# Normalised activations turned by DMA instead of TensorE, chunk bounds in two PSUM banks, and a planner that keeps TensorE in one array shape

## The chip, the cores and the metric

The kernel runs on one core of a Trainium2 chip. The metric is device time in microseconds, median of three runs: 303.88 us before (303.85 to 304.03). One further execution was profiled; it took 304.15 us, of which the trace covers a span of 302.4 us.

## What is computed

Attention with chunk selection, then a gated feed-forward layer (FFN). For q, k, v of shape 4 x 8 x 768 x 64 (batch, heads, tokens, head width), keys are cut into 24 chunks of 32. An upper bound of each query's score with each chunk is made from the chunk's smallest and largest keys:

```
ub = sum_d max(q * k_min, q * k_max)          # per query and chunk
top = the 6 chunks of largest ub, among those not after the query's own
scores = where(chunk in top and key <= query, q k^T / 8, -1e9)
attn = softmax(scores); x = attn v            # heads side by side: 3072 tokens x 512
xn = x / rms(x) * g
out = (silu(xn Wg) * (xn Wv)) Wo              # Wg, Wv: 512 x 1536, Wo: 1536 x 512
```

## The kernel before, in words

Work is cut into 12 blocks: a batch b and a third m of its 768 tokens, so 256 tokens with all 8 heads. `ORDER` lists them (m = 0 of all batches first, m = 2 last); "block 3" is the entry with index 3. Each block goes through:

- loads of k, q, v by DMA on SyncE's queue (SP, `load_qk`, `load_v`; the first block also on ScalarE's);
- `job`, once for each group of four heads: VectorE (DVE) turns k and q in 32x32 pieces, casts go to ScalarE (ACT) or GpSimd (POOL), DVE reduces k to chunk minima and maxima, which are placed in a block-diagonal matrix BD;
- `pick`: TensorE (PE) multiplies BD with q (`upper`, L562, 64x64 array tiles), DVE turns the bounds back (L583), finds the sixth largest and makes a mask; the mask enters the scores as a further matmul (L731);
- scores (L720, four 32-row tiles of the array), exponentials on ACT (L770), causal triangles on POOL (L740), values (L796, whole array), normalisation by the softmax sum on DVE (L815) into `xnat`, 128 tokens x 512;
- `norm`: squares and their sum on ACT (L832), the inverse root on POOL (L838, L840), a scaling by it on DVE or ACT (L848, L850), then the turn so that the 512 features lie on partitions: PE transposes into PSUM (L860, eight 128x128 blocks for 256 tokens), and a copy to `xsT` that multiplies by g, one value per partition (DVE L873 or ACT L869);
- `ffn`: gate and value matmuls (L904, 96 of 256 columns per block), tanh and products on ACT, DVE and POOL, the projection (L941, 24 of 512 columns), the output copy and its store on SP (L963).

PSUM holds two "S" tiles of two banks each, for scores (both are taken by one score operation) and bounds (one), and four "F" banks for everything else. Weights are loaded on POOL's queue in thirds. `HELD` makes the loads of blocks 2 and 3 wait for given thirds of the weights, so that these are not slowed.

The order of all this is not written out. Every operation is recorded with an engine, an assumed duration, what it reads, writes and takes from a pool of buffers, and a due time (`pri`, from `due_attn` and `due_ffn`: block number times `PACE`, attention `LEAD` ahead). `Plan.run` then walks through assumed time; on each engine it takes the operation that can start first, by due time among equals, and emits it. So each engine's instruction order is fixed when the program is built; on the chip each engine runs its list in order and waits where a semaphore is not there yet. Where the planner expects TensorE to wait before 60 us of its time, it puts in matmuls that do nothing but keep it busy (`fill`, L1008), called fillers below. `flex` operations may go to one of two engines, as the planner finds better.

Of the kernel before, what the change touches and what calls it, by code (L numbers as in the profile page):

```python
# [114 lines left out]
class Plan:  # L115
# [3 lines left out]
    SHARES = ("scale", "relu", "bd0", "bd1", "dk", "mk")  # L119
    PATIENT = {}  # L120
    RESERVED = ("hh",)
# [38 lines left out]
    def run(self, in_order=(), fill=None):  # L160
# [62 lines left out]
        while todo:  # L223
            best = None
            for e, c in cand.items():
                if not c:
                    continue
                rows = [(est(o, e), o) for o in c]
                rows = [(t, o) for t, o in rows if t is not None]
                if not rows:  # L230
                    continue
                t0 = max(at[e], min(t for t, o in rows))
                now = sorted(((t, o) for t, o in rows if t <= t0 + 1e-9),
                             key=lambda r: (r[1].pri, r[1].seq))
                t, o = now[0]
                if e in self.PATIENT:
                    soon = [r for r in rows if r[0] <= t0 + self.PATIENT[e]]
                    for t, o in now + sorted(soon, key=lambda r: (r[1].pri, r[1].seq)):
                        end = t + o.alts[e][0] - 0.1
                        if not any(t < r[0] < end and r[1].pri < o.pri - 10 for r in soon):  # L240
                            break
                    t0 = max(t0, t)
                if best is None or (t0, o.pri) < (best[0], best[1].pri):
                    best = (t0, o, e)
# [63 lines left out]
def kernel(  # L308
# [48 lines left out]
    buffers("qT", 3, [P, 2, BLK], FP32)  # L357
    buffers("kb", 20, [P, 2, BLK], BF16)
    buffers("VX", 20, [P, 2, 4, D + 1], BF16)
    buffers("qb", 5, [P, 2, BLK], BF16)  # L360
# [5 lines left out]
    buffers("mto", 3, [P, NG, 4, CH], BF16)  # L366
    buffers("pt", 6, [P, 4, 512], BF16)
    buffers("rden", 3, [P, 4], FP32)
# [14 lines left out]
    chunkrow = sb.tile([P, S], BF16, name="chunkrow")  # L383
    rmsg = sb.tile([P, NP], FP32, name="rmsg")
    eps6 = sb.tile([P, 1], FP32, name="eps6")
    mhalf = sb.tile([P, 1], FP32, name="mhalf")
# [13 lines left out]
    assert sorted(ORDER) == [(b, m) for b in range(B) for m in range(NBLK)]  # L400
    PACE, LEAD = 22.5, 70
    MARGIN = 2.0
    FIRST = 8
    SPLIT = {0, 1}
    APART = {0, 1}
    PACKED = {0, 1, 2}
# [67 lines left out]

    HELD = {2: (("wg", 1), ("wg", 1)), 3: (("wo", 0), ("wo", 1))}

# [25 lines left out]
    def loads_due(i, n):  # L502
        return -500 + 10 * i + n if i < 2 else due_attn(i) - 30 + n

    def load_v(i):
        b, m = ORDER[i]
        key = ("vraw", b, m)
        for e in range(2):
            t0 = BLK * m + P * e
            dma(f"load v{b}{m}{e}", "SP", v[b, :, t0:t0 + P, :].rearrange("a p d -> p a d"),  # L510
                lambda e=e: at(key)[:, e].rearrange("p g a d -> p (g a) d"),
                64, 0.023 if i < 2 else 0.019, loads_due(i, 2), writes=[key],
                takes=[(key, "vraw")] if e == 0 else (),
                behind=[HELD[i][1]] if i in HELD and e == 0 else ())

# [15 lines left out]
    def pick(i, gs):  # L531
# [8 lines left out]
        ub, ubn, m8, mk, mtd, mto = (  # L540
            ("ub", b, m, g0), ("ubn", b, m), ("m8", b, m), ("mk", b, m), ("mtd", b, m), ("mto", b, m))
        new = g0 == 0
# [7 lines left out]
        def bank():  # L550
            return at(ub)[:, :, 0:n * 32 * nj].rearrange("p h (g n) -> p g h n", g=n)

        def upper():
            for k_, g in enumerate(gs):
# [71 lines left out]
    def job(i, g):  # L626
# [117 lines left out]
        for kg in [m] + list(range(m)):  # L744
# [40 lines left out]
        for s in range(2):  # L785
# [36 lines left out]
    def norm(i, toks, base):  # L822
# [14 lines left out]
        def rms():  # L837
# [43 lines left out]
    def ffn(i):  # L881
# [6 lines left out]
        for toks, h0 in pieces:  # L888
# [22 lines left out]
            plan.op(f"tanh{U}.{hp}", "ACT", 0.48, 0.6, lambda th=th, gp=gp: SE.activation(  # L911
                out=at(th), in_=at(gp), func=ACT.Tanh, scale=0.5), pri - 20, reads=[gp], writes=[th],
                takes=[(th, "th")])
            plan.op(f"tg{U}.{hp}", "DVE", 0.6, 0.69, lambda th=th, gp=gp, tg=tg:
                    VE.scalar_tensor_tensor(  # L915
                        out=at(tg), in0=at(th), scalar=1.0, in1=at(gp), op0=ALU.add,
                        op1=ALU.mult), pri - 40, reads=[th, gp], writes=[tg], takes=[(tg, "tg")])
            if (i, h0 // 2) in DIRECT:
                plan.op(f"hh{U}.{hp}", "DVE", 0.6, 0.69, lambda tg=tg, vp=vp, hh=hh: VE.tensor_tensor(
                    out=at(hh), in0=at(tg), in1=at(vp), op=ALU.mult), pri - 30, reads=[tg, vp],  # L920
                    writes=[hh], takes=[(hh, "hh")])
# [7 lines left out]
        for s in whole:  # L929
# [8 lines left out]
            def project(h0, h1, s=s, op=op, part=part):  # L938
                for ht in range(h0, h1):
# [12 lines left out]
            o = plan.op(f"project{i}.{s}+", "PE", 0.216 * 2, 0.216 * 2 + 0.17,  # L952
                        lambda project=project: project(last, NHT), pri - 20,
                        reads=[part(NHT - 1)[0], op], writes=[op])
# [5 lines left out]
                    out=at(ob), in0=at(op), scalar1=0.5, scalar2=None, op0=ALU.mult))},  # L960
                pri - 20, reads=[op], writes=[ob], takes=[(ob, "osb")])
            r0 = b * S + BLK * m + P * s
# [79 lines left out]
```

## Time and profile before

| what | value |
|---|---|
| median of three runs | 303.88 us |
| profiled execution | 304.15 us, span 302.4 us |
| TensorE (PE) | 290.9 us busy, 4703 matmuls |
| VectorE (DVE) | 206.7 us busy, 540 instructions |
| ScalarE (ACT) | 219.8 us busy, 396 instructions |
| GpSimd (POOL) | 165.9 us busy, 293 instructions |
| turns on PE (L860) | 96 matmuls |
| feed-forward matmuls (L904) | 1216, of 256 or 128 columns |
| projection matmuls (L941) | 288 (264 in the trace) |
| bytes moved by DMA | 30.62 MB |

Busy time is the union of an engine's instructions. Matmuls overlap in the array: one row may show 0.27 us while the next starts 0.11 us later, so what a group of matmuls takes is read from start to start. A line of groups reads: source line, engine, operation, output tile <- inputs, shapes, count | busy us, mean ns of one | idle time of the engine just before them and who ended it. A line of waits reads: engine, tile, line <- who ended the wait: total us, times, longest.

### The profile page before, as it was taken

Reading aid. Unit: us, or ns where it says so; the run is one execution under the profiler, and the core shown is the slowest. Engines: PE = TensorE matmul, PEld = TensorE weight load, DVE = VectorE, ACT = ScalarE, POOL = GpSimd, SP = SyncE. Lnnn points to the kernel's source line nnn. Section 1 sums busy time; section 2 is a strip of 40 time slices with the busy share of each in tenths; the row PEclk is TensorE's granted clock in tenths of the full one; section 3 lists DMA queues with packets and bytes.
Section 4 is the critical chain, followed back from the end, with each engine's and each line's share of the span. In section 5 each row is a group of like instructions: output and inputs, shape, how many; then the busy total and the mean of one; then the engine's idle time right before and its main releaser. Section 6 shows DMA issues by size and latency. Waiting matters only on the chain.

```text
span 302.4 us, 11439 instructions
## 1 busy us (share of the span) xinstructions
PE 290.9 (96%) x4703; PEld 222.5 (74%) x4732; DVE 206.7 (68%) x540; ACT 219.8 (73%) x396; POOL 165.9 (55%) x293
## 2 busy tenths in 40 slices
PE   8989899998999999999999999999999999999994
PEld 8656696757958867885886787788588688598671
DVE  7994896888999999899889343384456335256250
ACT  3587886778976899898795896798667498476240
POOL 4797586856684888678779365246414043123130
PEclk9999999999999999999999999999999999999998
DMA  8999994775765657586540100100010110110101
GB/s 190 236 208 229 237 204 113 155 203 124 190 158 145 146 113 183 124 167 165 138 99 4 72 2 2 70 4 3 2 72 2 37 38 2 37 37 0 69 2 69
DMA packets 74835, 30.62 MB, mean 101 GB/s; under 512 B 65568, under 2 KB 70176, under 8 KB 74784
## 3 DMA queue, kind: packets, MB, share of 16 engines
q1 hardware_dynamic: 69184, 24.66, 33.6%
q0 software_dynamic: 4752, 4.72, 9.3%
q8 instruction: 37, 0.61, 0.8%
q10 hardware_dynamic: 848, 0.53, 0.6%
q14 instruction: 14, 0.11, 0.1%
HBM read 28.31 MB, written 6.29 MB: 114 GB/s over the span
## 4 chain that ended last, share of the span: by engine, by line
PE 77%; DMA 9%; DVE 3%; POOL 3%; ACT 2%; issue 2%; SPq 2%; ACTq 0%; DVEq 0%; POOLq 0%
PE F L904 37%; PE F L941 17%; PE F L796 7%; PE S L720 7%; PE S L562 5%; DMA wg<-in_moe_w_gate_dram 4%; DMA kraw<-in_k_dram 3%; PE S L731 3%; DMA qraw<-in_q_dram 2%; SPq L422 2%; PE F L860 1%; POOL hh L926 1%; DVE qT L642 1%; POOL pt L740 1%; DVE kT L642 1%
## 5 line engine op out<-in xcount | busy, mean ns | idle before, releaser
L926 POOL TENSOR_TENSOR hh<-tg,vs 128x512 bf16<-128x512 bf16 x60 | 69.6, 1163 | 69.0 <-ACT vs L923 47.3
L770 ACT ACTIVATE pt<-S 128x1024 bf16<-128x1024 f32 (+3 forms) x104 | 87.2, 861 | 19.7 <-PE S L731 19.3
L915 DVE SCALAR_TENSOR_TENSOR tg<-th,F 128x512 bf16<-128x512 bf16 x72 | 48.8, 681 | 41.1 <-ACT th L911 40.5
L904 PE MATMUL F<-xsT,wv 128*128 128x256 bf16 (+1 forms) x608 | 74.8, 267 | 1.4 <-DMA wv<-in_moe_w_val_dram 0.6
L904 PE MATMUL F<-xsT,wg 128*128 128x256 bf16 (+1 forms) x608 | 74.5, 267 | 0.5 <-DVE xsT L873 0.5
L941 PE MATMUL F<-wo,hh 128*128 128x512 bf16 x264 | 65.2, 379 | 1.6 <-issue 0.3
L904 PEld LDWEIGHTS <-wv 128*128 128x128 bf16 x608 | 55.5, 98 | 9.7 <-issue 1.5
L904 PEld LDWEIGHTS <-wg 128*128 128x128 bf16 x608 | 55.5, 98 | 8.6 <-issue 0.6
L911 ACT ACTIVATE th<-F 128x512 bf16<-128x512 f32 x72 | 43.3, 603 | 12.6 <-PE F L904 12.2
L941 PEld LDWEIGHTS <-hh 128*128 128x128 bf16 x288 | 26.5, 98 | 27.6
L923 ACT ACTIVATE vs<-F 128x512 bf16<-128x512 f32 x60 | 35.9, 612 | 9.4 <-PE F L904 8.2
L740 POOL TENSOR_SCALAR_AFFINE_SELECT pt<-pt 128x512 bf16<-128x512 bf16 x48 | 30.9, 649 | 12.1 <-ACT pt L770 11.5
L720 PE MATMUL S<-qb,kb 32*128 32x256 bf16 (+1 forms) x800 | 32.8, 253 | 0.0
L657 DVE TENSOR_REDUCE kx<-kT 128x16 f32<-128x512 f32 x48 | 30.4, 666 | 0.0
L796 PE MATMUL F<-VX,pt 128*128 128x65 bf16 x672 | 26.3, 194 | 0.6 <-POOL pt L740 0.3
L796 PEld LDWEIGHTS <-pt 128*128 128x128 bf16 x672 | 24.1, 98 | 3.3 <-issue 1.3
L720 PEld LDWEIGHTS <-kb 32*128 32x128 bf16 x800 | 13.6, 92 | 14.2 <-issue 13.5
L959 DVE TENSOR_SCALAR osb<-F 128x512 f32<-128x512 f32 x12 | 8.2, 688 | 23.1 <-PE F L941 23.1
L832 ACT ACTIVATE junk<-xnat 128x512 bf16<-128x512 bf16 x24 | 15.1, 627 | 10.1 <-DVE xnat L815 8.8
L731 PE MATMUL S<-mtd,chunkrow 32*128 32x128 bf16 (+2 forms) x384 | 20.3, 203 | 0.0
L815 DVE TENSOR_TENSOR xnat<-F,rden 128x256 bf16<-128x256 f32 x48 | 19.6, 415 | 0.9
L731 PE MATMUL S<-mto,chunkrow 32*128 32x128 bf16 (+2 forms) x384 | 20.0, 203 | 0.1
(61 smaller groups left out, 359.1 us busy)
## 6 DMA issues: line engine op xcount, KB each, us to landing
vraw<-in_v_dram SPq DMA_DIRECT2D x24, 256.0 KB, 4.0
out_dram<-osb SPq DMA_DIRECT2D x24, 256.0 KB, 2.2
kraw<-in_k_dram SPq DMA_DIRECT2D x72, 64.0 KB, 2.9
qraw<-in_q_dram SPq DMA_DIRECT2D x72, 64.0 KB, 2.4
wg<-in_moe_w_gate_dram POOLq DMA_DIRECT2D x3, 512.0 KB, 10.8
wv<-in_moe_w_val_dram POOLq DMA_DIRECT2D x3, 512.0 KB, 12.6
wo<-in_moe_w_out_dram POOLq DMA_DIRECT2D x3, 512.0 KB, 17.0
kraw<-in_k_dram SPq DMA_DIRECT2D x10, 128.0 KB, 4.7
```

Source lines behind the costliest of these rows:

```text
L657: plan.op(f"ext{n}{J}", "DVE", 0.585, 0.67, lambda n=n, op=op: VE.tensor_reduce(out=at(kx)[:, n], in_=at(kT).rearrange("p h (c t) -> p h c ...
L720: TE.matmul(s[a // 2][:, a % 2, c0:c0 + q1 - q0], kbt[r, t, ks], qbt[r, t, q0:q1], start=(t == 0), stop=(t == 1 and not mask), skip_group_ ...
L731: TE.matmul(o, chunkrow[r, BLK * kg + P * e:BLK * kg + P * (e + 1)], mv, start=False, stop=(d == 1), skip_group_check=True)
L740: GE.affine_select(out=d, in_=d, compare_op=ALU.is_ge, fill=0.0, base=0, pattern=[[0, 4], [1, P]], channel_multiplier=-1)
L770: lambda pt=pt, hs=hs, c0=c0, c1=c1, x=sc[hp]: SE.activation(out=at(pt)[:, hs, c0:c1], in_=at(x)[:, :, c0:c1], func=ACT.Exp, scale=SCALE), ...
L796: TE.matmul(o[:, a, :], p_[:, a, off:off + P], vt[:, e, a, :], start=(kb_ == 0 and a == 0), stop=(kb_ == nkb - 1 and a == 3), skip_group_c ...
L904: TE.matmul(at(p_)[:, n * W:(n + 1) * W], w[:, g, ht * P:(ht + 1) * P], at(xT)[:, g, x0:x0 + W], start=(g == 0), stop=(g == NP - 1), skip_ ...
L911: plan.op(f"tanh{U}.{hp}", "ACT", 0.48, 0.6, lambda th=th, gp=gp: SE.activation(out=at(th), in_=at(gp), func=ACT.Tanh, scale=0.5), pri - 2 ...
L915: VE.scalar_tensor_tensor(out=at(tg), in0=at(th), scalar=1.0, in1=at(gp), op0=ALU.add, op1=ALU.mult), pri - 40, reads=[th, gp], writes=[tg ...
L923: plan.op(f"vcopy{U}.{hp}", "ACT", 0.48, 0.6, lambda vs=vs, vp=vp: SE.activation(out=at(vs), in_=at(vp), func=ACT.Copy), pri + 0.1, reads= ...
L926: plan.op(f"hh{U}.{hp}", "POOL", 1.11, 1.16, lambda tg=tg, vs=vs, hh=hh: GE.tensor_tensor(out=at(hh), in0=at(tg), in1=at(vs), op=ALU.mult) ...
L941: TE.matmul(at(op)[:], at(key)[:, o:o + P], wo[:, ht, :], start=(ht == 0), stop=(ht == NHT - 1))
```

## The change

- From block 3 on (`BYDMA`), `norm` no longer turns on PE. DVE multiplies `xnat` by the inverse root and by g in one instruction; for that g is broadcast over all partitions into a new tile `gB` by a DMA. Then, for each 128 tokens, SP issues a DMA that transposes `xs` into `xsT`. The PSUM tile of the turn and the copy out of it are gone for these blocks.
- The bounds go to two F banks, one for each half of the heads, instead of one S tile; DVE turns them back in two instructions.
- Planner: after a bounds or score operation (`mode` other than "full"), operations of such a mode are preferred by 60 us of due time over those that use the whole array (`STICK`); `PATIENT` lets DVE wait up to 0.6 us for something more urgent; `PACE`, `LEAD` and several due times are different.
- Block 1's two head groups are picked together (`APART`). Block 3's k and q loads wait for the second instead of the first third of Wo. The weights' issues follow a planned operation of block 0 and stay in their order.
- Fewer buffers of kb, VX and pt.

In the instruction lists of the two programs: PE's turn matmuls go from 96 to 24, fillers of 512 columns from 38 to 46, and TensorE changes between array shapes 121 instead of 130 times, 7 of them directly between scores and bounds. DVE gets 18 of the new scalings, loses 6 of the old and 3 copies to `xsT`; ACT loses 12 scalings and 24 copies. SP issues 18 transposes and one load more.

```diff
     SHARES = ("scale", "relu", "bd0", "bd1", "dk", "mk")
-    PATIENT = {}
+    PATIENT = {"DVE": 0.6}
+    STICK = 60
...
                 now = sorted(((t, o) for t, o in rows if t <= t0 + 1e-9),
                              key=lambda r: (r[1].pri, r[1].seq))
+                if e == "PE" and mode not in (None, "full") and self.STICK:
+                    now.sort(key=lambda r: (r[1].pri - (0 if r[1].mode == "full" else self.STICK), r[1].seq))
...
-    buffers("kb", 20, [P, 2, BLK], BF16)
-    buffers("VX", 20, [P, 2, 4, D + 1], BF16)
+    buffers("kb", 18, [P, 2, BLK], BF16)
+    buffers("VX", 19, [P, 2, 4, D + 1], BF16)
...
-    buffers("pt", 6, [P, 4, 512], BF16)
+    buffers("pt", 5, [P, 4, 512], BF16)
...
+    gB = sb.tile([P, DM], FP32, name="gB")
...
-    PACE, LEAD = 22.5, 70
+    PACE, LEAD = 23.0, 60
     MARGIN = 2.0
     FIRST = 8
+    FROM = 3
+    GATES = {"0": "dk(0, 0, 0)", "1": "dk(0, 0, 0)", "2": "dk(0, 0, 0)", "o": "dk(0, 0, 0)"}
     SPLIT = {0, 1}
-    APART = {0, 1}
+    APART = {0}
+    BYDMA = set(range(FROM, len(ORDER)))
...
-    HELD = {2: (("wg", 1), ("wg", 1)), 3: (("wo", 0), ("wo", 1))}
+    HELD = {2: (("wg", 1), ("wg", 1)), 3: (("wo", 1), ("wo", 1))}
...
-        return -500 + 10 * i + n if i < 2 else due_attn(i) - 30 + n
+        return -500 + 10 * i + n if i < 2 else due_attn(i) - 20 + n
...
-            ("ub", b, m, g0), ("ubn", b, m), ("m8", b, m), ("mk", b, m), ("mtd", b, m), ("mto", b, m))
+            [("ub", b, m, g0, h) for h in range(2)], ("ubn", b, m), ("m8", b, m), ("mk", b, m), ("mtd", b, m), ("mto", b, m))
...
-                            TE.matmul(bank()[64 * c:64 * (c + 1), k_, hp],
+                            TE.matmul(bank()[hp][64 * c:64 * (c + 1), k_],
...
-                    upper, base + 3, reads=reads, writes=[ub], takes=[(ub, "S")])
+                    upper, base + 3, reads=reads, writes=ub, takes=[(x, "F") for x in ub])
...
-        plan.op(f"ubn{tag}", "DVE", turned, turned + 0.08, lambda: VE.transpose(out=flat(ubn), in_=bank()),
-                base + 3, reads=[ub], writes=own_(ubn), takes=takes(ubn, "ubn"))
+        def back():
+            for h in range(2):
+                VE.transpose(out=flat(ubn)[:, :, h], in_=bank()[h])
...
-                pri = base + (5 if masked else -4)
+                pri = base + (2 if masked else -4)
...
-            pri = base + (-4 if i in SPLIT and not s else 9)
+            pri = base + (-4 if i in SPLIT and not s else 6)
...
+        if i in BYDMA:
+            for s in toks:
+                xn, xs, tt = ("xnat", b, m, s), ("xs", i, s), 2 * blk + s
+
+                def weigh(eng, xn=xn, xs=xs, tt=tt):
+                    return lambda: eng.scalar_tensor_tensor(
+                        out=at(xs), in0=at(xn), scalar=ri_all[:, tt:tt + 1], in1=gB[:],
+                        op0=ALU.mult, op1=ALU.mult)
+
+                flex(f"scale{i}{s}", {"DVE": (0.67, 0.83, weigh(VE))}, base,
+                     reads=[xn, ("ri", *U), "gB"], writes=[xs], takes=[(xs, "xs")])
+                o = plan.op(f"across{i}{s}", "SP", 1.2, 1.2, lambda s=s, xs=xs: SY.dma_start_transpose(
+                    out=at(xT)[:, :, P * s:P * (s + 1)], in_=at(xs)), base - 40,
+                    reads=[xs] + ([xT] if s else []), writes=[xT + (s,)], takes=[] if s else [(xT, "xsT")])
+                o.dma = (32, 0.035, True)
+            return
...
-            pri = base + 6 + s
+            pri = base + 10 + s
...
+        if i == 2:
+            dma("gB", "SP", moe_rms_g.rearrange("(o n) -> o n", o=1).broadcast_to([P, DM]), lambda: gB[:], 8, 0.1,
+                due_attn(2) - 20, writes=["gB"], behind=[("wv", 2)])
...
-            for o in plan.ops:
-                if o.dma and o.eng == "POOL":
-                    o.after.append(first_dk[0])
+            named = {o.name: o for o in plan.ops}
+            for x, y in GATES.items():
+                for nm in ("wg", "wv") if x != "o" else ("wo",):
+                    named[nm + (x if x != "o" else "0")].deps.append(named[y])
+            chain = [o for o in plan.ops if o.dma and o.eng == "POOL"]
+            for x, y in zip(chain, chain[1:]):
+                y.after.append(x)
```

Four due times of the FFN's vector operations and of the output copy differ too.

More of the change, by code (lines that the diff above doesn't have):

```diff
@@ L511, in load_v @@
                 lambda e=e: at(key)[:, e].rearrange("p g a d -> p (g a) d"),
-                64, 0.023 if i < 2 else 0.019, loads_due(i, 2), writes=[key],
+                64, 0.023 if i < 2 else 0.019, loads_due(i, 2 if i != 1 else 2), writes=[key],
                 takes=[(key, "vraw")] if e == 0 else (),
@@ L550, in bank @@
         def bank():
-            return at(ub)[:, :, 0:n * 32 * nj].rearrange("p h (g n) -> p g h n", g=n)
+            return [at(x)[:, 0:n * 32 * nj].rearrange("p (g n) -> p g n", g=n) for x in ub]
         def upper():
@@ L582, in pick @@
         turned = ((0.37 if m else 0.17), (0.65 if m else 0.25))[n - 1]
-        plan.op(f"ubn{tag}", "DVE", turned, turned + 0.08, lambda: VE.transpose(out=flat(ubn), in_=bank()),
-                base + 3, reads=[ub], writes=own_(ubn), takes=takes(ubn, "ubn"))
+        def back():
+            for h in range(2):
+                VE.transpose(out=flat(ubn)[:, :, h], in_=bank()[h])
+        plan.op(f"ubn{tag}", "DVE", turned + 0.08, turned + 0.16, back,
+                base + 3, reads=ub, writes=own_(ubn), takes=takes(ubn, "ubn"))
         def bar():
@@ L911, in ffn @@
             plan.op(f"tanh{U}.{hp}", "ACT", 0.48, 0.6, lambda th=th, gp=gp: SE.activation(
-                out=at(th), in_=at(gp), func=ACT.Tanh, scale=0.5), pri - 20, reads=[gp], writes=[th],
+                out=at(th), in_=at(gp), func=ACT.Tanh, scale=0.5), pri - 10, reads=[gp], writes=[th],
                 takes=[(th, "th")])
@@ L916, in ffn @@
                         out=at(tg), in0=at(th), scalar=1.0, in1=at(gp), op0=ALU.add,
-                        op1=ALU.mult), pri - 40, reads=[th, gp], writes=[tg], takes=[(tg, "tg")])
+                        op1=ALU.mult), pri - 20, reads=[th, gp], writes=[tg], takes=[(tg, "tg")])
             if (i, h0 // 2) in DIRECT:
                 plan.op(f"hh{U}.{hp}", "DVE", 0.6, 0.69, lambda tg=tg, vp=vp, hh=hh: VE.tensor_tensor(
-                    out=at(hh), in0=at(tg), in1=at(vp), op=ALU.mult), pri - 30, reads=[tg, vp],
+                    out=at(hh), in0=at(tg), in1=at(vp), op=ALU.mult), pri - 60, reads=[tg, vp],
                     writes=[hh], takes=[(hh, "hh")])
@@ L952, in ffn @@
             o = plan.op(f"project{i}.{s}+", "PE", 0.216 * 2, 0.216 * 2 + 0.17,
-                        lambda project=project: project(last, NHT), pri - 20,
+                        lambda project=project: project(last, NHT), pri - 30,
                         reads=[part(NHT - 1)[0], op], writes=[op])
@@ L960, in ffn @@
                     out=at(ob), in0=at(op), scalar1=0.5, scalar2=None, op0=ALU.mult))},
-                pri - 20, reads=[op], writes=[ob], takes=[(ob, "osb")])
+                pri - 0, reads=[op], writes=[ob], takes=[(ob, "osb")])
             r0 = b * S + BLK * m + P * s
```

## The prediction

> **What bounds the kernel now.** I read the page's busy times and slices first, then busy time by stretch, the waits of TensorE, the costliest groups, and TensorE's own timeline. The busy line and two slices:
>
> ```profile
> PE 290.9 (96%) x4703; PEld 222.5 (74%) x4732; DVE 206.7 (68%) x540; ACT 219.8 (73%) x396; POOL 165.9 (55%) x293
> PE   8989899998999999999999999999999999999994
> DVE  7994896888999999899889343384456335256250
> ```
>
> TensorE (PE) is busy nearly always and its granted clock stays at full, so the span is PE's queue from the first microsecond on. DVE is a near second up to about 150 us and half empty after. By stretch (columns: PE, PEld, DVE, ACT, POOL busy, clock, DMA share, GB/s):
>
> ```profile
> 0.00:46.34 46.34, 41.59 (x679) 32.70 (x684) 37.02 (x89) 31.82 (x71) 32.95 (x88) 1.00 1.13 216
> 72.88:121.10 48.22, 47.85 (x796) 36.92 (x798) 45.06 (x127) 40.20 (x74) 35.83 (x62) 1.00 0.63 153
> 121.10:170.00 48.90, 48.53 (x929) 37.84 (x936) 42.53 (x129) 39.21 (x67) 35.02 (x59) 1.00 0.47 109
> 269.00:298.20 29.20, 29.04 (x222) 21.34 (x222) 12.89 (x24) 13.18 (x26) 6.65 (x7) 1.00 0.05 19
> ```
>
> PE idles 4.75 us in the opening (46.34 less 41.59) and only some tenths per stretch afterwards; 4.2 us (298.2 to 302.4) are the last output copy and its store. Work taken from PE after the opening is therefore worth its full time; work moved to DVE costs nothing unless DVE falls behind PE. PE's longest waits show no resource that is short:
>
> ```profile
> PE F L860 <- ACT xs L850: 0.7, 2, 0.5
> PE F L904 <- DMA wv<-in_moe_w_val_dram: 0.6, 1, 0.6
> PE F L904 <- DVE xsT L873: 0.5, 1, 0.5
> ```
>
> **PE work removed: the turns.** Nine of ten eight-matmul turns (blocks 3 to 11) go. What one is worth is read from starts on PE's timeline, not from durations, which overlap:
>
> ```profile
> 78.30 0.61 PE L860 MATMUL F<-ident,xs 128*128 128x128 bf16 x8
> 78.74 1.04 PE L904 MATMUL F<-xsT,wv 128*128 128x256 bf16 x8
> ...
> 83.11 1.04 PE L904 MATMUL F<-xsT,wg 128*128 128x256 bf16 x8
> 83.98 1.04 PE L904 MATMUL F<-xsT,wv 128*128 128x256 bf16 x8
> 84.95 0.40 PE L720 MATMUL S<-qb,kb 32*128 32x256 bf16 x8
> ```
>
> 78.74 less 78.30 is 0.44 us: 9 x 0.44 = **-4.0 us**.
>
> **Changes of array shape.** FFN, projection, values and turns use the whole array, scores 32-row tiles, chunk bounds 64x64. Eight FFN matmuls take 0.87 us (83.11 to 83.98), but 0.97 when scores follow (83.98 to 84.95): a change costs 0.10. Leaving a bounds operation costs 0.55 instead of 0.44 (93.96 to 94.51, 93.52 to 93.96), also 0.1. Counted over both programs' PE order there are 130 changes before and 121 after; all 130 have the whole array on one side, while 7 of the 121 go directly between scores and bounds, which this trace never shows. If a direct change were free the gain is 1.6 us, if it cost double 0.2; I take it like the others: 9 x 0.10 = **-0.9 us**.
>
> **Fillers.** The planner puts idle-time matmuls (L1008) where it foresees PE waiting. Both programs have 86 narrow ones; of the 512-column ones there are 38 before and 46 after. Before the first FFN matmul 27 become 25, behind it 11 become 21: block 1's bounds are now one operation behind a third FFN piece, and the gaps ahead of that piece are filled. Ten of them ran from 13.94 to 16.19, so 0.22 each: 8 x 0.22 = **+1.7 us**, all in the opening. Bounds: 0 if PE would have waited less and the idle of 4.75 us shrinks with it, +3 if unplanned waits come on top.
>
> **Sum.** -4.0 - 0.9 + 1.7 = -3.2 us. All else on PE (1216 FFN, 288 projection, 672 values, 800 scores, 768 mask, 384 bounds matmuls) is the same in number. The profiled execution took 304.15 us (span 302.4 and 1.75 around it), so 300.95; the median lies 0.27 below it at 303.88, so **300.7 us**.
>
> **What is costed at nothing, and its cover.** *DVE.* It gains 18 weighted scalings (bf16 and fp32 from SBUF). Nearest row is tg, the same instruction and shape with one operand in PSUM:
>
> ```profile
> L915 DVE SCALAR_TENSOR_TENSOR tg<-th,F 128x512 bf16<-128x512 bf16 x72 | 48.8, 681 | 41.1 <-ACT th L911 40.5 <-POOL pt L740 0.4
> L848 DVE TENSOR_SCALAR xs<-xnat,ri_all 128x512 bf16<-128x512 bf16 x7 | 3.7, 525 | 2.6 <-POOL ri_all L840 2.6
> L873 DVE TENSOR_TENSOR xsT<-F,rmsg 128x1024 bf16<-128x1024 bf16 x3 | 3.7, 1222 | 0.5 <-PE F L860 0.5
> L869 ACT ACTIVATE xsT<-F,rmsg 128x256 bf16<-128x256 bf16 x28 | 11.0, 478 | 3.2 <-PE F L860 3.2
> ```
>
> 18 x 0.68 = 12.2; it loses six scalings (3.1) and three xsT copies (3.7), so +5.4; two half-size back-transposes for one cost 0.1 to 0.2 more in each of 12 blocks (128 columns take 313 ns, 512 take 710), +2; small operations moved to and from POOL and ACT, about +1. DVE: 207 to 215 of 300. By place it matters more: multiplying each engine's instructions, in order, by their start-to-start times, from the last normalisation of block 4 to that of block 7 I get 64 us for DVE against 64 for PE; before, in its worst three blocks (4 to 6), 75 against 78, and there the trace lets PE idle only 0.4 us between 100 and 150. So DVE is level with PE there, not ahead. The single xs row of 1.24 us (median 0.35) shows a scaling can be held up; at that length the six scalings of those blocks cost 3.3 us more. *ACT* loses 12 scalings and 24 xsT copies and gains 12 casts and 3 output copies: about -13 us, no risk.
>
> *PSUM.* Bounds take two of four F banks instead of one of two S pairs. Scores may overlap them; FFN has two banks meanwhile, with DVE to empty the others. 0, at worst 0.1 in each of 11 blocks.
>
> *Loads.* POOL casts VX (0.6) ahead of the first weight's issue: 0 to 0.6, inside the fillers. Block 3's k and q wait for wo's second third: wg's second third landed at 24.4 and wo's first at 38.4, four transfers later, 3.5 us each, so k issues near 42 and not 38.4; gB, waiting for wv's last third (about 35), goes ahead of it and fits. Block 3's bounds stand 16 FFN and 10 projection matmuls later on PE (1.75 + 2.16 = 3.9 us), the same distance. Block 0's stores now stand on SP ahead of block 4's k: these start near 58.5 instead of 52.2, land by 67, and DVE needs about 5.5 us (two k and two q turns at 0.7, four reductions at 0.6) to have block 4's bounds ready; those come on PE near 78.6. Cover 6 us; past it PE's bounds wait.
>
> **The transposes.** 18 SBUF-to-SBUF DMAs of 128 KB on SP, each waiting for its scaling; queued behind them on SP are the next v and k loads or stores, which have blocks of time. The place with least cover is block 11. After the last values matmul (268.98) the scalings started at 272.2: 3.2 us. Now both run on DVE, so the first is ready at 3.9 and the second at 4.6. PE's own work between a block's last values and its first FFN matmul, by its order, is 13.1 us for block 3, 12.2 for block 4, 10.5 for block 11 and 16 or more elsewhere. So 5.9 us are there for landing. Nearest rows:
>
> ```profile
> vraw<-in_v_dram SPq DMA_DIRECT2D x24, 256.0 KB, 4.0
> out_dram<-osb SPq DMA_DIRECT2D x24, 256.0 KB, 2.2
> kraw<-in_k_dram SPq DMA_DIRECT2D x72, 64.0 KB, 2.9
> ```
>
> By these, 2.2 to 4.0 us, up to twice that behind queued loads: covered. [...] I take the rows: of the 24 stores, twice as large, the slowest took 4.9 us, and no loads run beside block 11's.
>
> **Rivals.** (1) *Slower: transposes land late.* [...] Against: rows. With L us per transpose, one after the other, block 11 waits 3.9 + 2L - 10.5, block 4 the same less 12.2, block 3 less 13.1; the sum eats the 3.2 us from L = 4.5 on. [...] (2) *DVE becomes the bound in blocks 5 to 7*: for, 64 against 64; against, 75 against 78 did no harm. Held-up scalings give back 1.5 to 3.3: 302.2 to 304. (3) *The opening is better than its fillers*: they merely replace waits and 1.7 to 2 us of the 4.75 idle go: 298.7 to 299.2. (4) *It does not pay*: PE's gain returns as waits for F banks (1.1) and unplanned waits in the opening (1.5 to 3): 303.3 to 304.8.
>
> **How the numbers follow.** A kernel's time is told from no change at about 0.2%, so 303.27 to 304.49 is "same". The sum holds, 299.2 to 302.2: 0.55; rival 1: 0.15; rival 2: 0.13; rival 3: 0.10; rival 4: 0.07. Faster: 0.55 + 0.10 + half of rival 2 = 0.71. Same: the rest of rival 2's upper end and half of rival 4 = 0.08. Slower: 0.21. The range 298.6 to 305.5 leaves out the far end of rival 1 and a little of rival 3; the likeliest case's own range is 299.2 to 302.2.
>
> **What would show it.** Right: 24 turn matmuls left; the 18 transposes at 2 to 4 us to landing; no wait of FFN matmuls on xsT; PE busy near 287 with its idle time about 11; the last normalisation about 5 us earlier while 24 more FFN matmuls follow it. Wrong: FFN waiting for the transposes at blocks 3, 4 or 11; bounds or scores waiting for DVE between 115 and 165 us; the point where block 2's bounds start (46.34 before, 48 by my sum) later than 50.

## The result, and the profile after

The changed kernel takes 303.36 us (303.10 to 303.81); the kernel before, on the same chip, 303.95 (303.85 to 304.13). The ratio is 0.9981, 95% interval 0.9964 to 0.9999: faster by 0.2%, where the sum said 1.1%. The profiled execution took 303.81 us with a span of 302.1. So of the 3.2 us that the sum took off, 0.6 came. Below, first the busy line and the slices of VectorE (DVE) on the page of after, then busy time by stretch (columns as in the prediction; the first stretch ends about where block 2's bounds start, at 47.05).

```profile
PE 288.5 (96%) x4643; PEld 219.6 (73%) x4668; DVE 220.7 (73%) x564; ACT 213.2 (71%) x371; POOL 162.0 (54%) x273
DVE  5997995978897899999999999296254256267250
```

```profile
0.00:47.00 47.00, 42.09 (x687) 32.40 (x692) 39.58 (x95) 30.43 (x66) 32.52 (x83) 1.00 1.12 216
72.88:121.10 48.22, 47.13 (x792) 36.30 (x793) 43.16 (x125) 38.97 (x69) 32.06 (x50) 1.00 0.63 137
121.10:170.00 48.90, 47.26 (x863) 36.61 (x864) 46.94 (x133) 39.96 (x67) 30.84 (x48) 1.00 0.64 142
```

TensorE's (PE) work fell as told, but between 73 and 170 us it now idles 2.73 us (1.09 + 1.64) where it idled 0.74 before, and DVE is busy 46.9 of 48.9 us in the second of these stretches, 42.5 before. The waits of PE that are new, and the groups behind them:

```profile
PE F L931 <- DVE tg L942: 2.4, 5, 0.8
PE S L731 <- ACT qb L660: 1.4, 1, 1.4
PE F L569 <- DVE tg L942: 0.6, 1, 0.6
```

```profile
L861 DVE SCALAR_TENSOR_TENSOR xs<-xnat,ri_all,gB 128x512 bf16<-128x512 bf16 x18 | 21.1, 1212 | 2.7 <-POOL ri_all L851 2.7
L942 DVE SCALAR_TENSOR_TENSOR tg<-th,F 128x512 bf16<-128x512 bf16 x72 | 48.9, 681 | 31.0 <-ACT th L938 30.2 <-POOL kx L673 0.3
L953 POOL TENSOR_TENSOR hh<-tg,vs 128x512 bf16<-128x512 bf16 x60 | 71.5, 1197 | 45.4 <-ACT vs L950 32.6 <-DVE tg L942 11.4 <-ACT pt L781 0.8
```

PE's feed-forward (FFN) matmuls (L931) and bounds (L569) wait 3.0 us for `tg`; before, 0.2 us is the only wait for it that the list of waits has. Two of the six waits (0.52 us at 37.52, 0.27 at 59.28) come ahead of the first weighted scaling (78.8); the other four, 2.1 us, come behind it. The weighted scalings (L861) are the cause to suspect: 1.21 us each, not 0.68, while `tg` (L942), the row from which the 0.68 came, is still at 0.68. Six of the 18 took 0.71 to 0.75 us, four 1.05 to 1.12, eight 1.55 to 1.64. One place in the timeline of after (start, duration, engine, line; the lines between these are left out):

```profile
156.71 0.65 DVE L942 SCALAR_TENSOR_TENSOR tg<-th,F 128x512 bf16<-128x512 bf16 x1
157.28 2.31 DVE L861 SCALAR_TENSOR_TENSOR xs<-xnat,ri_all,gB 128x512 bf16<-128x512 bf16 x2
157.41 1.03 PE L931 MATMUL F<-xsT,wg 128*128 128x256 bf16 x8 [0.76 <-DVE tg L942]
157.51 1.53 POOL L953 TENSOR_TENSOR hh<-tg,vs 128x512 bf16<-128x512 bf16 x1
159.51 1.27 DVE L942 SCALAR_TENSOR_TENSOR tg<-th,F 128x512 bf16<-128x512 bf16 x2
160.24 0.54 PE L569 MATMUL F<-qT,BD 64*64 64x128 f32 x10 [0.56 <-DVE tg L942]
```

Two scalings keep DVE for 2.31 us. GpSimd's (POOL) product of the FFN (`hh`) starts beside the first and takes 1.53 us instead of 1.16 (the mean of before); the second scaling has to wait for it. The `tg` behind them starts at 159.51, so the F bank that it empties comes free late, and the bounds, which now take F banks, start 0.56 us late.

What the operations took on PE from block 2's bounds on, from the start of each to the start of the next (so waits are in it), in us; the last two columns are experiments told below:

| | before | after | scaling on 2 columns | products on 2 columns |
|---|---|---|---|---|
| turns | 4.91 | 0.46 | 0.46 | 0.46 |
| FFN | 113.07 | 114.15 | 112.86 | 114.06 |
| bounds | 17.43 | 18.63 | 17.67 | 17.82 |
| scores, masks | 31.12 | 32.39 | 30.91 | 30.81 |
| values | 22.16 | 22.00 | 22.00 | 22.01 |
| projection | 63.11 | 63.31 | 63.31 | 63.31 |
| idle among these | 2.49 | 4.58 | 2.16 | 2.99 |

The turns give 4.45 us; FFN, bounds and scores take 3.55 of it back.

### The profile page after: what moved, and what is told of

Its sections match the earlier page's. It is cut to its first block, busy times and chain, and to the rows that moved or that the text cites. A ratio compares the mean times of both kernels' runs of the same rounds, so it can differ in the third digit from the quotient of the medians.

```text
span 302.1 us, 11334 instructions
## 1 busy us (share of the span) xinstructions
PE 288.5 (96%) x4643; PEld 219.6 (73%) x4668; DVE 220.7 (73%) x564; ACT 213.2 (71%) x371; POOL 162.0 (54%) x273
## 4 chain that ended last, share of the span: by engine, by line
PE 72%; DVE 9%; DMA 7%; ACT 4%; issue 3%; SPq 2%; POOL 1%; ACTq 0%; DVEq 0%; POOLq 0%
PE F L931 33%; PE F L968 18%; PE S L731 6%; PE F L807 6%; PE F L569 5%; DMA wv<-in_moe_w_val_dram 3%; DVE xs L861 3%; DMA qraw<-in_q_dram 2%; PE S L742 2%; SPq L429 2%; DVE tg L942 2%; PE F L1042 1%; DVE kx L668 1%; ACT junk L843 1%; DVE qT L653 1%
## 5 line engine op out<-in xcount | busy, mean ns | idle before, releaser
L953 POOL TENSOR_TENSOR hh<-tg,vs 128x512 bf16<-128x512 bf16 x60 | 71.5, 1197 | 45.4 <-ACT vs L950 32.6
L931 PE MATMUL F<-xsT,wg 128*128 128x256 bf16 (+1 forms) x608 | 74.8, 267 | 2.4 <-DVE tg L942 1.9
L931 PE MATMUL F<-xsT,wv 128*128 128x256 bf16 (+1 forms) x608 | 74.7, 267 | 0.9 <-DVE tg L942 0.5
L942 DVE SCALAR_TENSOR_TENSOR tg<-th,F 128x512 bf16<-128x512 bf16 x72 | 48.9, 681 | 31.0 <-ACT th L938 30.2
L931 PEld LDWEIGHTS <-wg 128*128 128x128 bf16 x608 | 55.7, 98 | 10.6 <-issue 3.4
L931 PEld LDWEIGHTS <-wv 128*128 128x128 bf16 x608 | 55.1, 98 | 9.3 <-issue 1.5
L751 POOL TENSOR_SCALAR_AFFINE_SELECT pt<-pt 128x512 bf16<-128x512 bf16 x48 | 31.5, 661 | 36.9 <-ACT pt L781 36.3
L807 PEld LDWEIGHTS <-pt 128*128 128x128 bf16 x672 | 24.8, 98 | 4.8 <-issue 0.8
L807 PE MATMUL F<-VX,pt 128*128 128x65 bf16 x672 | 27.2, 194 | 0.6 <-DVE ubn L599 0.4
L861 DVE SCALAR_TENSOR_TENSOR xs<-xnat,ri_all,gB 128x512 bf16<-128x512 bf16 x18 | 21.1, 1212 | 2.7 <-POOL ri_all L851 2.7
L984 ACT ACTIVATE osb<-F 128x512 f32<-128x512 f32 x15 | 8.7, 593 | 18.1 <-PE F L968 18.1
L826 DVE TENSOR_TENSOR xnat<-F,rden 128x256 bf16<-128x256 f32 x48 | 20.0, 423 | 1.2
```

Source lines behind the costliest of these rows:

```text
L751: GE.affine_select(out=d, in_=d, compare_op=ALU.is_ge, fill=0.0, base=0, pattern=[[0, 4], [1, P]], channel_multiplier=-1)
L807: TE.matmul(o[:, a, :], p_[:, a, off:off + P], vt[:, e, a, :], start=(kb_ == 0 and a == 0), stop=(kb_ == nkb - 1 and a == 3), skip_group_c ...
L931: TE.matmul(at(p_)[:, n * W:(n + 1) * W], w[:, g, ht * P:(ht + 1) * P], at(xT)[:, g, x0:x0 + W], start=(g == 0), stop=(g == NP - 1), skip_ ...
L942: VE.scalar_tensor_tensor(out=at(tg), in0=at(th), scalar=1.0, in1=at(gp), op0=ALU.add, op1=ALU.mult), pri - 20, reads=[th, gp], writes=[tg ...
L953: plan.op(f"hh{U}.{hp}", "POOL", 1.11, 1.16, lambda tg=tg, vs=vs, hh=hh: GE.tensor_tensor(out=at(hh), in0=at(tg), in1=at(vs), op=ALU.mult) ...
```

## The experiments

Each expectation says what its letters stand for; A is nearly always that the sum holds but for the weighted scalings on DVE. Ratios are to the kernel before on the same chip, with a 95% interval. First those that keep the changed kernel's order on every engine, so that one thing alone differs.

**Scaling without g (e1).**

```diff
-                    return lambda: eng.scalar_tensor_tensor(
-                        out=at(xs), in0=at(xn), scalar=ri_all[:, tt:tt + 1], in1=gB[:],
-                        op0=ALU.mult, op1=ALU.mult)
+                    return lambda: eng.tensor_scalar(
+                        out=at(xs), in0=at(xn), scalar1=ri_all[:, tt:tt + 1], scalar2=None, op0=ALU.mult)
```

> The changed kernel with every engine's order kept, and the weighted scaling of blocks 3 to 11 replaced by a plain scaling: the product with g is left out. Theory A (DVE is late because its 18 scalings take 1.21 us each and not 0.68, and TensorE waits for it): a scaling takes 0.35 to 0.7, TensorE's waits for tg fall from 3.0 us to under 1.5, time 301.3 to 302.4. Theory B (the new order of score and bounds operations, with bounds in the F banks, costs what the turns save): 303.0 to 303.6, waits as before.

300.81 us, ratio 0.9890 (0.9855 to 0.9926): a little faster than A expected. PE waits 1.5 us for `tg`. The scaling's mean, 0.80 us, is above what was expected, because beside a product of GpSimd (POOL) the plain scaling takes 1.16 to 1.33 us too; those products stay at 1.16 in the mean. Its row among the groups:

```profile
L861 DVE TENSOR_SCALAR xs<-xnat,ri_all 128x512 bf16<-128x512 bf16 x18 | 13.7, 802 | 2.7 <-POOL ri_all L851 2.7
```

**Scaling on 2 of 512 columns (e2).**

```diff
-                        out=at(xs), in0=at(xn), scalar=ri_all[:, tt:tt + 1], in1=gB[:],
+                        out=at(xs)[:, 0:2], in0=at(xn)[:, 0:2], scalar=ri_all[:, tt:tt + 1], in1=gB[:, 0:2],
```

> The changed kernel with every engine's order kept, and the weighted scaling done on 2 of 512 columns: the rest is left out. Theory A in its form that length and a wait for POOL both count: the instruction itself is under 0.1 us, and what is left above that is waiting for POOL's product (mean 0.3 to 0.6); time 300.8 to 302.0. If no wait for POOL exists, the mean is under 0.1 us. Theory B: 303.0 to 303.6.

300.90 us, ratio 0.9884 (0.9853 to 0.9915). Both give the predicted gain, 1.1%, with all that the sum counted still in place. In e2's profile it is 247.2 us from block 2's bounds to the end of PE, against 251.8 before: -4.65, where the sum said -4.9 (turns and array shapes) from that point on. (The opening of that execution is 1.2 us longer than that of after, with a wait of 1.6 us for a third of Wv.) PE's wait for `tg`, and the line of the scalings by source (durations min/median/max, ns):

```profile
PE F L931 <- DVE tg L942: 0.8, 2, 0.5
L861 DVE SCALAR_TENSOR_TENSOR xs<-xnat,ri_all,gB x18: 207/364/1201, 80.0 to 266.9; 128x2 bf16<-128x2 bf16 x18
```

The 0.8 us are the two waits ahead of the first scaling; the four behind it are gone. An instruction on two columns that takes 0.21 us at one time (more than the 0.1 expected) and 1.20 at another spends most of the 1.20 waiting, not working.

**For what it waits: the products on 2 of 512 columns (e18).** The scalings stay whole.

```diff
+            nx = 2 if i > 2 else 512
...
-                out=at(hh), in0=at(tg), in1=at(vs), op=ALU.mult), pri - 40, reads=[tg, vs],
+                out=at(hh)[:, 0:nx], in0=at(tg)[:, 0:nx], in1=at(vs)[:, 0:nx], op=ALU.mult), pri - 40, reads=[tg, vs],
```

> The changed kernel in its own order, with GpSimd's gated products of blocks 3 to 11 cut to 2 of 512 columns (the rest of each product is left out); the weighted scalings stay whole. Theory A (the scalings are long because GpSimd's product holds them, and this is what TensorE pays): scalings at 0.72 to 0.85 us instead of 1.21, waits for tg below 1.5 us instead of 3.0, 300.6 to 301.6 us. Rival (the scaling is slow by itself, with an fp32 operand beside bf16): scalings still above 1.0 us, 302.8 to 303.6.

300.00 us, ratio 0.9856 (0.9824 to 0.9887); mean 0.95, median 0.75. The groups' row and PE's wait:

```profile
L861 DVE SCALAR_TENSOR_TENSOR xs<-xnat,ri_all,gB 128x512 bf16<-128x512 bf16 x18 | 16.3, 947 | 5.2 <-POOL ri_all L851 5.2
PE F L931 <- DVE tg L942: 1.6, 3, 0.9
```

The two scalings beside products still whole (of block 2) took 1.56 and 1.64 us, those beside the causal triangle (L751) or a cast up to 1.11, the others 0.74. Mean and wait are a little above what was expected because of those triangles and casts; the time is a little below. The rival, a scaling slow by itself, falls. But the edit also takes 40 us of work off POOL (its products take 31.2 us in all, not 71.5), so the gain need not all be the hold's.

**Both engines alone and together (probe p1).** Behind the end of the changed kernel, six instructions of each kind, alone and on both engines at once. `weighed` is the new scaling on DVE, `product` the FFN's product on POOL; the pair shown runs at once. The probe's own time (348 us) says nothing.

```diff
+    for _ in range(6):
+        weighed(xc[:], ha[:], gB[:])
+    for _ in range(6):
+        product(hb[:], ha[:])
...
```

> The changed kernel with work behind its end: six weighted scalings alone, six of POOL's products alone, then both at once; then the tg form (second operand in PSUM) beside the products, the scaling with g in bf16 beside them, and a plain bf16 scaling beside them. If DVE and POOL exclude each other where DVE reads two operands from SBUF: alone 0.7 and 1.15, together each instruction waits for the other's, 1.8 to 1.9 between starts on both; tg beside POOL stays at 0.68; bf16 g behaves like fp32 g. If the long scalings are due to fp32 g alone: 1.2 alone, and no difference together. Time itself says nothing (about 40 us more).

The timeline behind the end (durations are of all six): each alone, both at once, `tg`'s form with its operand in PSUM, and the plain scaling from bf16.

```profile
298.64 4.68 DVE L1056 SCALAR_TENSOR_TENSOR xs<-xnat,ri_all,gB 128x512 bf16<-128x512 bf16 x6
303.47 7.29 POOL L1059 TENSOR_TENSOR hh<-xs,vs 128x512 bf16<-128x512 bf16 x6 [10.47 <-DVE xs L1056]
310.79 9.52 DVE L1056 SCALAR_TENSOR_TENSOR xs<-hh,ri_all,gB 128x512 bf16<-128x512 bf16 x6 [7.47 <-POOL hh L1059]
310.83 8.93 POOL L1059 TENSOR_TENSOR hh<-hh,vs 128x512 bf16<-128x512 bf16 x6
320.50 4.29 DVE L1071 SCALAR_TENSOR_TENSOR tg<-tg,F 128x512 bf16<-128x512 bf16 x6
337.44 7.49 DVE L1080 TENSOR_SCALAR tg<-tg,ri_all 128x512 bf16<-128x512 bf16 x6
```

Alone 0.78 us per scaling and 1.22 per product; together one of each every 1.59 and 1.49 us, where 1.8 to 1.9 was expected. With g in bf16 it is the same 1.59 and 1.49, so the type of g isn't the reason. `tg`'s form is as fast beside POOL (0.72 from start to start) as anywhere: its second operand comes from PSUM. That is the difference between the scaling and the row that priced it. (`tg` also has a constant where the scaling has one value per partition. The trace of after tells against that as the reason: beside POOL, DVE's products with two inputs in SBUF and no such value, L680 and L673, take up to 1.03 and 1.12 us where they take 0.18 alone, while none of the 72 `tg`, nor of the 48 products of L826, which also read PSUM, takes more than 0.69 and 0.43.) The plain scaling, 1.25 here beside POOL and 0.3 to 0.4 alone in the kernel, waits too, though it has one input in SBUF; but POOL's products beside it keep 1.22. The weighted scaling both waits and makes them wait.

The other runs are planned anew, so the order differs on all engines.

**The change without the DMA turns (e3), and with them from block 8 on (e4).**

```diff
-    FROM = 3
+    FROM = 12      # e4: 8
```

> The changed kernel without its DMA turns: all blocks are turned on TensorE, everything else of the change stays and the planner lays it out anew. Theory A: the rest of the change alone is worth little, -0.9 for fewer changes of array shape and +1.7 in the opening, so 304 to 305, and no scaling above 0.8 us on average. Theory B: the rest of the change is what costs, 305.5 to 307.

> The changed kernel with DMA turns only from the ninth block on, where DVE is half empty. Theory A: four turns off TensorE give -1.8 without waits for DVE, the rest of the change +0.8 to 0 as in the run without DMA turns, so 302.3 to 303.2. Theory B: above 304.

306.15 us, ratio 1.0059 (1.0041 to 1.0077), and 304.56, 1.0014 (0.9996 to 1.0031): both as theory B said. The other parts by themselves make the kernel slower by 1.9 us (306.15 less 304.22, the kernel before on that chip), not by the sum's 0.8 (1.7 less 0.9); PE waits for ACT's copy to `xsT` (1.1) and for `tg` (1.3). Four blocks' turns bring 1.4 to 1.6 back (4 x 0.44 = 1.8). A's range for e4 was missed because it took the rest of the change to cost less.

**The turns alone, on the kernel before: with the weighted scaling (e5), and with g multiplied by POOL ahead of a plain scaling (e10b, the edit shown under e12).** `FROM`, `BYDMA`, `gB`, its load, the new branch of `norm` and the fewer buffers; nothing else of the change.

> The kernel before with one part of the change: blocks 3 to 11 turned by DMA (with gB, the weighted scaling and the smaller pools), bounds, planner settings and due times as before. Theory A (turns off TensorE give 4.0 to 4.4, scalings held up by POOL give part back): 301.0 to 302.7, TensorE waiting 1 to 3 us more for tg than before. Theory C (the whole change has the same balance because its parts need each other): no faster than the change, 303.3 or more.

> The kernel before, with its planner and its bounds tile, and of the change only the turns by DMA from block 3 on; g is multiplied by GpSimd ahead of a one-operand scaling on DVE. All computed, planned anew. Theory A (the turns are worth 4.0 us and only the long scalings took that back): 300.0 to 301.5 us. Theory D (before's due times and the S tile for the bounds don't go with the DMA turns): 303.5 to 306.5, as with the weighted scalings.

305.97 us, 1.0062 (1.0027 to 1.0097), and 305.56, 1.0055 (1.0027 to 1.0083). In e5 PE waits for scalings on ACT (1.8), `pt` (1.2), `qb` (1.2), bounds (0.9), `tg` (1.4); in e10b 2.1 us for one transpose, behind which the granted clock is 0.50 for 3.4 us, and 1.6 for `pt`, with DVE's scalings at 0.67. Both profiled executions (307.07 and 307.49 us) are slower than the medians, so not every execution need have these waits. So on the old due times the turns by DMA lose, whether the scalings are long or short: A falls for these two.

**The planner told the scalings' true length (e6); the scaling on ACT and POOL (e8); g multiplied by POOL while ACT squares (e12).**

```diff
-                flex(f"scale{i}{s}", {"DVE": (0.67, 0.83, weigh(VE))}, base,
+                flex(f"scale{i}{s}", {"DVE": (1.2, 1.3, weigh(VE))}, base,
```

> The changed kernel with one number of the planner changed: the scaling is taken to last 1.2 us and not 0.67, as measured. If the loss is only that the order was laid out for a scaling half as long, a new order avoids most waits: 301.5 to 302.5. If it is the time on DVE as such, or the hold itself: 303 to 303.8, as the change.

```diff
+                plan.op(f"scale{i}{s}", "ACT", 0.62, 0.72, lambda xn=xn, xs=xs, tt=tt: SE.activation(
+                    out=at(xs), in_=at(xn), func=ACT.Copy, scale=ri_all[:, tt:tt + 1]), base,
+                    reads=[xn, ("ri", *U)], writes=[xs], takes=[(xs, "xs")])
+                plan.op(f"weigh{i}{s}", "POOL", 1.11, 1.16, lambda xs=xs: GE.tensor_tensor(
+                    out=at(xs), in0=at(xs), in1=gB[:], op=ALU.mult), base, reads=[xs, "gB"], writes=[xs])
```

> The changed kernel with the weighted scaling taken off DVE: ACT multiplies by the inverse root, POOL by g. Theory A: DVE loses 21 us, TensorE's waits for tg nearly go; ACT gains 13 and POOL 21 us, both have room; 300.5 to 302. Theory B: 303 or more.

```diff
+                plan.op(f"weigh{i}{s}", "POOL", 1.11, 1.16, lambda xn=xn, xs=xs: GE.tensor_tensor(
+                    out=at(xs), in0=at(xn), in1=gB[:], op=ALU.mult), base - 5,
+                    reads=[xn, "gB"], writes=[xs], takes=[(xs, "xs")])
+                plan.op(f"scale{i}{s}", "DVE", 0.3, 0.38, lambda xs=xs, tt=tt: VE.tensor_scalar(
+                    out=at(xs), in0=at(xs), scalar1=ri_all[:, tt:tt + 1], scalar2=None, op0=ALU.mult), base,
+                    reads=[xs, ("ri", *U)], writes=[xs])
```

> The scaling of blocks 3 to 11 in two steps: GpSimd multiplies the normalised x by g while ScalarE squares it, and DVE then scales by the inverse root with one SBUF operand; all computed, planned anew. Theory A (what is lost are DVE's long scalings, and GpSimd has room for 18 products of 1.15 us): 300.8 to 301.9 us, DVE's scalings at 0.3 to 0.8 us. Theory D (a new layout brings its own waits, as in the three plans before): 303 to 305, with the scalings short all the same.

e6: 303.51 us, 0.9997 (0.9968 to 1.0025): no gain, as the second theory said; PE waits 1.7 us for `pt` instead. e8: 303.29, 0.9983 (0.9964 to 1.0002): DVE is at 205.4 us, yet `tg` is waited for (1.7) and the turned bounds (1.0); B's range. e12: 300.88, 0.9884 (0.9843 to 0.9924): everything computed and faster than both kernels, as A said; but the order is new, and how much of this is the order's is not known. In e12 the groups' rows, DVE's scaling and POOL's product by g, and PE's wait:

```profile
L868 DVE TENSOR_SCALAR xs<-xs,ri_all 128x512 bf16<-128x512 bf16 x18 | 10.6, 628 | 2.6 <-POOL ri_all L851 2.5
L865 POOL TENSOR_TENSOR xs<-xnat,gB 128x512 bf16<-128x512 bf16 x18 | 20.6, 1163 | 8.2 <-DVE xnat L826 8.2
PE F L935 <- DVE tg L946: 0.8, 2, 0.5
```

**Without the shape preference (e7); the same without g (e16, in e7's order); with e12's scaling (e15); the preference alone on the kernel before (e17).**

```diff
-    STICK = 60
+    STICK = 0
```

> The changed kernel without the preference for operations of the same array shape (STICK 0), planned anew. Theory A (the preference saves what the sum gave to array shapes, 0.9 us, and costs nothing): 304.0 to 304.6 us. Theory D (the preference holds FFN work back and costs more in waits than it saves; it is a part of why everything but the DMA turns made the kernel 2.2 us slower than before): 301.5 to 303.0. If the plan's layout alone is worth 1 to 3 us either way, it can lie anywhere from 302 to 306.

> The kernel without the shape preference, its order kept, with g left out of the scalings of blocks 3 to 11 (plain scaling, one SBUF operand). Theory A (the long scalings cost time wherever they stand): 298.5 to 299.5 us, 1.7 to 2.7 below the kernel without the preference. Theory D (without the preference the scalings have cover, and the preference's loss is this loss of cover): 300.6 to 301.4, no better than without the preference alone, and no better than the changed kernel without g, 300.8.

> Both improvements together, all computed: no shape preference, and GpSimd multiplies by g ahead of a one-operand scaling on DVE. Theory A (two separate losses): 298.4 to 299.6 us. Theory D (one and the same loss, of DVE's cover): 300.3 to 301.5.

> The kernel before with the shape preference alone, planned anew. Theory A (the preference saves array changes and does no harm by itself): 303.0 to 304.0 us. Theory D1 (it costs by itself, by holding back the FFN): 305 to 307. Theory D2 (it only hurts beside the new scalings): within 0.5 us of the kernel before.

e7: 301.17 us, 0.9894 (0.9865 to 0.9923), faster than either theory said. e16: 299.88, 0.9847 (0.9821 to 0.9874). e15: 302.17, 0.9928 (0.9903 to 0.9954), slower than either said. e17: 304.38, 1.0004 (0.9987 to 1.0022). The preference saves no change of array shape: 121, 7 of them direct, with and without it. Nor can a cost of it be told on the kernel before. In e7 the scalings are as long as in the changed kernel, and PE hardly waits for them (0.78 of the 0.9 us are again ahead of the first one):

```profile
L861 DVE SCALAR_TENSOR_TENSOR xs<-xnat,ri_all,gB 128x512 bf16<-128x512 bf16 x18 | 20.9, 1201 | 3.9 <-POOL ri_all L851 3.9
PE F L931 <- DVE tg L942: 0.9, 3, 0.5
```

Between 120 and 170 us DVE is busy 44.1 of 50 us in it, against 47.7 in the changed kernel. So what the length costs depends on where the order puts the scalings. Leaving out g there still gains 0.47 points of ratio, 1.4 us, where it gains 0.91 in the changed kernel's order: between the two theories, with 0.4 points of doubt either way in both figures (worked out from the intervals). And e12's and e7's gains don't add up (e15 is no faster than either).

**Bounds in an S tile again (e9); the old due times (e13).**

```diff
-                    upper, base + 3, reads=reads, writes=ub, takes=[(x, "F") for x in ub])
+                    upper, base + 3, reads=reads, writes=ub, takes=[(x, "S") for x in ub])
...
-    PACE, LEAD = 23.0, 60
+    PACE, LEAD = 22.5, 70
```

> The changed kernel with the bounds in one S tile again, as before, planned anew. Theory A (two F banks for the bounds cost FFN at most 0.1 us per block): 302.3 to 303.4 us. Theory D (the two F banks are what lets scores follow bounds at once; without them scores wait for the S tile): 304 to 306.

> The changed kernel with the due times' old constants (PACE 22.5, LEAD 70 in place of 23 and 60), planned anew; no instruction more or less. Theory A (only the amount of work counts): 303.0 to 303.8 us, like the changed kernel. Theory D (a plan's layout is worth as much as the change's parts): more than 0.8 us away from 303.4, with other waits of TensorE in the trace.

305.98 us, 1.0067 (1.0041 to 1.0092), and 306.64, 1.0081 (1.0054 to 1.0107). In e9 array changes are 127, one of them direct, and scores, masks and bounds wait 3.3 us for `pt` and `mtd`: the two F banks are the part that saves array changes, and the plan without them is 2.6 us slower than the changed kernel. e13 has not one instruction more of the reference's work and is 3.0 to 3.3 us slower (by ratios, by medians), but not through waits alone. Its stretches (columns as before, the sixth number in each row after the length is the granted clock):

```profile
34.00:38.00 4.00, 2.31 (x54) 1.80 (x52) 4.00 (x9) 2.91 (x6) 3.48 (x9) 1.00 1.21 197
38.00:42.00 4.00, 2.57 (x18) 1.87 (x18) 3.71 (x8) 1.34 (x4) 1.96 (x5) 0.51 1.22 197
42.00:46.00 4.00, 4.00 (x76) 2.85 (x77) 0.69 (x1) 2.33 (x4) 3.88 (x4) 0.63 1.13 233
```

PE idles 1.69 us in four, and the clock is 0.51 and 0.63 for the next eight: 0.49 x 4 + 0.37 x 4 = 3.4 us of full clock lost, an estimate, and an upper one, since PE idles 1.4 of the eight anyway. In e9's profiled execution it fell in the same way (0.72, 0.50, 0.92 from 88 to 100 us) after 1.11 us of idle time in four; that execution took 307.79 us, 1.8 more than the median.

## Why the prediction was wrong

**The direction and most terms were right, the size was not.** 303.36 lies inside the range, at the edge of "same", and far from 300.7.

**The step that failed** is "18 x 0.68 = 12.2", and with it that DVE's part is costed at nothing. It measured 21.1 us. The row was the nearest in instruction and shape, but not in where its operands lie: `tg` reads one from PSUM, the scaling two from SBUF. Beside POOL's products that decides, as the probe shows: 0.72 us for `tg`'s form, 1.59 for the scaling. The prediction did read the one row of before that shows a hold, the scaling of 1.24 us, but kept it for rival 2 and priced the sum without asking what stood beside it:

```profile
62.40 1.16 POOL L926 TENSOR_TENSOR hh<-tg,vs 128x512 bf16<-128x512 bf16 x1
62.46 1.24 DVE L848 TENSOR_SCALAR xs<-xnat,ri_all 128x512 bf16<-128x512 bf16 x1 [0.62 <-POOL ri_all L840]
```

That row is a plain scaling with one input in SBUF; e1 and the probe show the same wait (1.16 to 1.33 and 1.25 us beside a product).

The sentence "work moved to DVE costs nothing unless DVE falls behind PE" stands; that DVE would not fall behind is what failed. The scalings took 8.9 us more than the sum gave them (21.1 less 12.2), where DVE had little to spare (46.9 of 48.9 us busy), and one of the prediction's own signs of being wrong came: bounds waiting for DVE between 115 and 165 us (0.56 us at 160.24). How much such a length costs depends on the order: in e7, with the same length, PE waits 0.16 us for `tg` behind the first scaling, though leaving out g still gains 1.4 us (e16).

**Rival 2 was the right one, and got 0.13.** It named the place (blocks 5 to 7), the level race of DVE and PE there, 64 against 64, and a time of 302.2 to 304. "75 against 78 did no harm" was no reason against it, as after has 46.9 of 48.9 there. With the order kept, taking the length away gives 2.5 to 2.9 us (e1, e2: by medians, by ratios) and taking POOL's products away 3.4 to 3.8 (e18), each with about 1.2 us of doubt either way by the intervals, against the 2.7 missing.

**Turns: right.** -4.0; -4.45 measured, waits included. **Array shapes:** right in number (121); what they are worth by themselves can't be told apart, but turns and shapes together are -4.65 in e2 against -4.9. They come from the bounds' banks (127 without), not from the preference.

**Fillers and opening: half.** +1.7; block 2's bounds start 0.7 us later. Between 20 and 40 us PE's idle fell from 2.60 to 1.35 us, which is rival 3's mechanism; in the first ten it rose from 1.50 to 2.89. The order ahead of that point isn't the same, so these don't add up to the 0.7.

**Transposes: right.** 2.4 us to landing in the median, 4.2 at most, 1.2 of it on SP's sequencer, and no wait of PE in after. Rival 1 and the reach of the range above the sum, up to 305.5, rest in part on a time per transpose that no run shows; what the runs showed in its place are these 2.4 us and, in e5, 2.9 in the median. In e10b one block waited 2.1 us, so the cover is not there on every plan.

**Loads, PSUM:** nothing to see. The one longer wait of scores in the opening (1.4 us for `qb`) is also in e3, e1 and e7 at 0.9 to 1.2.

**What stays open.** The order-kept runs settle what the scalings cost in this order. Why e3, e5, e8, e10b and e15 are slower than their parts say is shown only as waits in new places (`pt`, `xsT`, bounds, casts), each time others; no single cause was found. A prediction that adds parts on a kernel whose order is planned anew is off by 1 to 3 us here, where the intervals of the measured times are 0.5 to 1.2 us either way; that e12 came out as expected may be luck in part.

## What to carry to other kernels

Take the price of an elementwise instruction from a row whose operands lie in the same memories (`tg` took 0.68 us with one operand in PSUM, the scaling 1.21 with both in SBUF), and ask what GpSimd does at that moment. On two engines that are level, time added on the second can be paid by the first (here 2.5 to 2.9 us, e1 and e2), unless the order covers it; so multiply by a constant vector where there is room and time (here on GpSimd ahead of the norm, e12, 300.88 us) rather than where it saves an instruction. When a planner lays out the order, change the operation with the order kept before believing any difference between two plans.

## What was not expected of the hardware

- The hold works both ways but is not a plain queue: 1.59 and 1.49 us per pair in the probe, where 0.78 + 1.22 = 2.00 was to be expected if each instruction kept the other out from start to end. In the kernel a scaling that starts first takes 0.74 and the product 1.53 instead of 1.16; one that starts after a product takes up to 1.64.
- In e13 and e9 PE idled 1.79 and 1.53 us, in pieces, in the four us before the granted clock fell to 0.50 for 6.8 us. PE was busy 5.5 and 6.6 us of these, so about 2.7 and 3.3 us were lost (an estimate: half of that time); a plan's waits then cost more than themselves. Idle time in four us doesn't decide it by itself: e6 idled 2.04 us (145.60 to 149.60) and e2 1.80 (19.40 to 23.40) with the clock at 1.00 there and behind. The changed kernel's own clock stayed at full (0.999 over the span).
